# Weights decoded where they land, two blocks per pass, in a Nyström-attention and two-MoE-layer kernel

## The chip, the cores and the metric

One core of one Trainium2 chip. The metric is device time in microseconds (us) of one execution. Engines are named as the profile names them: PE (TensorE matmuls), PEld (its weight loads), DVE (VectorE), ACT (ScalarE), POOL (GpSimd), SP (SyncE, which here issues most DMAs). Each engine runs its instructions in the order of its own queue and waits there for the others.

## What is computed

Attention with 32 landmarks over 4 batches of 8 heads (576 positions, 64 wide), then two feed-forward layers over the 2304 tokens that come out of it. The weights of both layers arrive as 64-bit floats.

```python
A  = softmax(q @ k_lm.T);  Bm = softmax(q_lm @ k_lm.T);  C = softmax(q_lm @ k.T)
Z  = Bm.T / (norm1(Bm) * norminf(Bm))
for _ in range(6):
    Z = 2 * Z - Z @ Bm @ Z
x  = (A @ Z @ C @ v)                      # to 2304 x 512
h  = x @ moe_w_in                         # 512 x 2048
x  = (h * tanh(softplus(h))) @ moe_w_out  # 2048 x 512
h  = x @ moe2_w_in                        # 512 x 1024
solu = h * softmax(h)
out = (layernorm(solu) * g_ln) @ moe2_w_out
```

## The kernel before

**Stages.** The kernel first computes attention for batch 0 alone (the start-up), then walks 64 *pairs* of hidden blocks of the first layer, and last the second layer in 18 token tiles. A chunk is 288 tokens; a hidden block is 128 of the 2048 hidden columns; a pair is two blocks of one chunk. For each pair `gemm1` makes h from A transposed (AT) and u, `mish` applies the activation on ACT, `gsplit` splits the result in a high and a low part (gh on ACT, gl on DVE), and `gemm2` adds gh and gl times the rows of w_out into y, three pairs later (`LAG = 3`). h takes 12 matmuls a pair and y 24. The pairs go chunk 0 first half (pairs 1 to 4), chunk 1 (5 to 12), chunk 0 second half (13 to 16), then chunk after chunk; chunks 0 and 1 need batch 0 and chunk 2, from pair 17, needs batch 1.

**u.** `u_step(b, s)` multiplies W, the 64-wide end of batch b's attention, into a quarter s (512 hidden columns) of w_in: 8 matmuls into two PSUM tiles, a copy of each on ACT and a subtraction of each on DVE.

**Decoding.** [...] A block is 128 rows of 512 values: 32 blocks of the first layer, 16 of the second. A block is loaded into a staging tile, and goes through one pass on ACT (L145, the exponent) and three on DVE (L155, L158, L161, the shift, the sign and the low bits); w_out then takes a copy on ACT (L117) and a subtraction on POOL (L120). A staging tile is loaded again only after the block in it is decoded, eight blocks later for the first 20 blocks and three later after that. In this kernel the steps of the decoder are called from `w1_tick`: a few in the start-up, where `PSEQ` says `d`, and the rest spread over the first `DT = 8.5` pairs.

**Attention.** Batch 0 runs in the start-up in the order of the list `PSEQ` (q, k: transposes; e: the 32 by 32 softmax and the Newton steps for Z; c: the C part; a: the A part; w: W). Sums of q and k over 18 positions, the landmarks, are DVE reductions (L299), except in an `early` batch and group, where 18 matmuls with `fold` per operand do it (L323). The other groups run from `tasks`, one step at a time from `slot`, five slots a pair, from the slot and at the spacing that `PLAN` gives. In the kernel before, batch 1 group 0 begins in the start-up (x in `PSEQ`) and then waits for slot 39, and its later steps wait for the decoder.

**Second layer.** The decoder of its weights (`w2`) starts two chunks before the end of the pairs, with three staging tiles, and the steps come from `tick`. `split_y` splits the 18 input tiles, the low part on POOL.

## Time and profile before

| | us |
|---|---|
| median of 3 runs | 710.8 |
| lowest and highest run | 710.26, 710.86 |
| the profiled execution | 710.08 |
| span of the profiled execution | 708.2 |
| PE busy | 661.7 |
| DVE busy | 422.2 |
| ACT busy | 339.6 |
| POOL busy | 90.2 |

The span runs from the first to the last instruction; 1.9 us lie outside of it. All stages share one chain, so an engine that is busy 60% over the whole span may be the limit of one stage and idle in another: the profile is to be read by stage. The mean granted TensorE clock is 0.968 of full speed.

### The profile page before, as it was taken

What the parts mean: (1) busy time and instruction counts of PE and PEld (TensorE: products, weight loads), DVE (VectorE), ACT (ScalarE), POOL (GpSimd) and SP (SyncE); (2) the same over time, 40 slices, a digit from 0 to 9 for tenths busy, and PEclk for the clock granted to TensorE, in tenths of its full rate; (3) what the DMA queues carried; (4) which work ended last, traced back from release to release, by engine and by line L of the source; (5) the groups of instructions that cost most, each with busy time, mean ns of one, the idle gap of its engine ahead of it and who ended that gap; (6) DMA issues with size and microseconds to landing.
All of it is one profiled execution on the core that took longest, in us unless ns stands there. A gap on an engine that the chain in (4) does not pass through costs nothing.

```text
span 708.2 us, 12192 instructions
## 1 busy us (share of the span) xinstructions
PE 661.7 (93%) x4720; PEld 560.8 (79%) x4720; DVE 422.2 (60%) x1103; ACT 339.6 (48%) x658; POOL 90.2 (13%) x79
## 2 busy tenths in 40 slices
PE   4945999899999999999999989999999999999997
PEld 2634788788579989689989689998788888888885
DVE  6689799966365534364235784292876565656560
ACT  2435655765358474463264663461643434343331
POOL 0022232421000101000001151000210101010000
PEclk9867999989899999999999999999999999999999
DMA  9948636214210220030010453131211111111011
GB/s 245 227 123 273 125 89 179 95 51 118 68 52 17 69 68 1 34 103 1 1 34 2 164 192 110 34 109 34 75 45 44 46 46 44 45 46 30 16 31 44
DMA packets 43352, 55.44 MB, mean 78 GB/s; under 512 B 7712, under 2 KB 34848, under 8 KB 43296
## 3 DMA queue, kind: packets, MB, share of 16 engines
q1 hardware_dynamic: 38112, 49.37, 25.2%
q10 hardware_dynamic: 5184, 5.31, 2.2%
q8 instruction: 37, 0.61, 0.4%
q14 instruction: 19, 0.16, 0.1%
HBM read 44.63 MB, written 10.03 MB: 77 GB/s over the span
## 4 chain that ended last, share of the span: by engine, by line
PE 77%; DVE 12%; ACT 3%; DMA 3%; issue 2%; POOL 2%; SPq 0%; ACTq 0%; POOLq 0%
PE h L601 25%; PE y L653 23%; PE po L601 14%; PE pa L592 2%; PE pt L960 2%; PE pa L307 2%; PE pa L474 2%; DVE cw L161 1%; DVE gl L640 1%; DVE cw L158 1%; DMA sg<-in_moe_w_in_dram 1%; PE pa L425 1%; PE pa L336 1%; PE pa L323 1%; PE pa L413 1%
## 5 line engine op out<-in xcount | busy, mean ns | idle before, releaser
L601 PE MATMUL h<-AT,u 128*128 128x288 f32 x768 | 125.2, 307 | 6.9 <-ACT s L630 3.2
L601 PEld LDWEIGHTS h<-AT,u 128*128 128x128 f32 x768 | 109.0, 193 | 24.9 <-ACT u L595 7.4
L640 DVE TENSOR_TENSOR gl<-s,gh 128x288 fp32r<-128x288 f32 x128 | 57.7, 485 | 78.0 <-PE y L653 42.3
L601 PE MATMUL h<-vi_h,yb 128*128 128x512 f32 x288 | 93.7, 396 | 1.0 <-POOL yb L120 0.6
L653 PE MATMUL y<-gh,wo_h 128*128 128x288 f32 x512 | 89.0, 304 | 3.1 <-ACT ye L659 3.1
L653 PE MATMUL y<-gh,wo_l 128*128 128x288 f32 x512 | 83.7, 297 | 0.0
L653 PE MATMUL y<-gl,wo_h 128*128 128x288 f32 x512 | 81.9, 297 | 0.0
L653 PEld LDWEIGHTS y<-gh,wo_h 128*128 128x128 f32 x512 | 73.6, 189 | 9.7 <-ACT ye L659 5.3
L653 PEld LDWEIGHTS y<-gh,wo_l 128*128 128x128 f32 x512 | 72.6, 188 | 2.2 <-issue 2.1
L653 PEld LDWEIGHTS y<-gl,wo_h 128*128 128x128 f32 x512 | 71.9, 188 | 1.8 <-issue 1.8
L638 ACT ACTIVATE gh<-s 128x288 fp32r<-128x288 f32 x128 | 50.2, 436 | 38.8 <-PE y L653 38.5
L630 ACT ACTIVATE s<-h 128x576 f32<-128x576 f32 x64 | 41.6, 650 | 50.4 <-PE h L601 44.0
L601 PEld LDWEIGHTS h<-vi_h,yb 128*128 128x128 f32 x288 | 54.0, 188 | 12.8 <-POOL yb L120 1.1
L601 PE MATMUL po<-vo_h,lh 128*128 128x512 f32 x144 | 57.2, 397 | 0.0
L601 PE MATMUL po<-vo_l,lh 128*128 128x512 f32 x144 | 56.6, 393 | 0.0
L601 PE MATMUL h<-vi_l,yb 128*128 128x512 f32 x144 | 56.5, 392 | 0.0
L601 PE MATMUL po<-vo_h,ll 128*128 128x512 f32 x144 | 56.2, 391 | 0.0
L120 POOL TENSOR_TENSOR yb<-y,yb 128x512 fp32r<-128x512 f32 x18 | 23.4, 1304 | 208.5 <-ACT yb L117 208.5
L928 DVE TENSOR_REDUCE st<-h 128x1 f32<-128x1024 f32 x18 | 22.0, 1224 | 35.2 <-PE h L601 24.0
L117 ACT ACTIVATE yb<-y 128x512 fp32r<-128x512 f32 x18 | 11.3, 631 | 59.8 <-issue 54.6
L936 ACT ACTIVATE e<-s,st 128x1024 f32<-128x1024 f32 x18 | 20.7, 1152 | 30.6 <-DVE st L935 30.6
L596 DVE TENSOR_TENSOR u<-pa,u 128x512 fp32r<-128x512 f32 x32 | 21.0, 685 | 23.9 <-ACT u L595 23.7
(233 smaller groups left out, 1032.1 us busy)
## 6 DMA issues: line engine op xcount, KB each, us to landing
st_h<-in_moe_w_in_dram SPq DMA_DIRECT2D x18, 256.0 KB, 8.4
yd<-ye ACTq DMA_DIRECT2D x32, 144.0 KB, 1.9
y<-yd SPq DMA_DIRECT2D x18, 256.0 KB, 3.1
out_dram<-ob SPq DMA_DIRECT2D x72, 64.0 KB, 1.7
stage<-in_moe_w_out_dram SPq DMA_DIRECT2D x8, 512.0 KB, 3.4
sg<-in_moe_w_in_dram SPq DMA_DIRECT2D x8, 512.0 KB, 4.2
sg<-in_moe_w_out_dram SPq DMA_DIRECT2D x8, 512.0 KB, 3.7
q<-in_q_dram SPq DMA_DIRECT2D x6, 576.0 KB, 4.7
```

The source lines that it names most:

```text
L120: G.tensor_tensor(out=lo, in0=c, in1=f(hi), op=ALU.subtract)
L307: PE.transpose(pt[:, o], flat(src[:, 2 * i:2 * i + 2]), ident)
L474: PE.matmul(pz[:, c0:2 * L], lhsT=Z1, rhs=X1[:, c0:], start=True, stop=True)
L592: PE.matmul(po[g][h * L:(h + 1) * L], lhsT=wb[b][r, g, h * L:(h + 1) * L], rhs=wi_half(s // 2)[r, h, o], start=True, stop=True)
L596: V.tensor_tensor(out=u[:, 1, g, o], in0=po[g], in1=f(u[:, 0, g, o]), op=ALU.subtract)
L601: PE.matmul(o, lhsT=a, rhs=b_, start=i == 0, stop=i == n - 1)
L630: A.activation(out=s, in_=h, func=AF.Mish)
L638: A.activation(out=gh[:, e], in_=s[:, e], func=AF.Copy)
L640: V.tensor_tensor(out=gl[:, e], in0=s[:, e], in1=f(gh[:, e]), op=ALU.subtract)
L653: PE.matmul(yb[s_][d][:, 0:N], lhsT=w_out(s, i + e)[:, 0, d * P:(d + 1) * P], rhs=r[:, e], start=i == i0 and e == k == 0, stop=i + 2 == i1 ...
L928: V.tensor_reduce(out=st[:, 0:1], in_=h, op=ALU.max, axis=AX.X)
L936: A.activation(out=e, in_=s, func=AF.Square, bias=st[:, 4:5], accum_out=st[:, 5:6])
```

## The change

Every weight is now loaded into the tile in which its decoded parts will stand. A *unit* is two blocks, 128 by 1024 values: 16 units in the first layer (8 of w_in, 8 of w_out) and 8 in the second. There are no staging tiles; the first 12 units of the first layer are loaded at the start with nothing to wait for (w_out's all, w_in's first four), and w_in's last four follow when batch 0 has left the memory that it borrows. q, k and v of batch 0 lie in four tiles instead of two, so v comes in 24 loads instead of 12, half as large.

A unit takes two passes on ACT (L143, the exponent; L145, which takes the fourth byte of each low word and leaves its upper three bits) and two on DVE (L153 and L162), all 1024 wide. w_out then takes one copy on ACT (L213) and one subtraction on DVE (L222). The result buffer `dc` (`cc` in the second layer) has two tiles. POOL takes no part in decoding or in `split_y` any more: DVE makes the low parts.

Batch 0 group 1 and batch 1 group 1 join the `early` ones, whose landmark sums are matmuls. Batch 1 leaves the start-up: group 0 starts at slot 3, group 1 at slot 22, both 1.6 slots apart, and neither waits for the decoder. The decoder is spread over `DT = 10` pairs. The second layer's first four units are loaded once all u steps are done and decoded at 0.6 steps per block; two of the others are loaded in the last chunk and two after it.

```diff
-        if eng is None:
-            A.activation(out=hi, in_=c, func=AF.Copy)
-        else:
-            eng.tensor_copy(out=hi, in_=c)
-        G.tensor_tensor(out=lo, in0=c, in1=f(hi), op=ALU.subtract)
+    def split(hi, lo, c, eng=V):
+        A.activation(out=hi, in_=c, func=AF.Copy)
+        eng.tensor_tensor(out=lo, in0=c, in1=f(hi), op=ALU.subtract)
...
-            elif s == 1:
-                V.tensor_scalar(out=w, in0=w, scalar1=3, scalar2=0x7FFFFFF8,
-                                op0=ALU.logical_shift_left, op1=ALU.bitwise_and)
-            elif s == 2:
-                V.scalar_tensor_tensor(out=w, in0=t[:, :, :, 1], scalar=0x80000000, in1=w,
-                                       op0=ALU.bitwise_and, op1=ALU.bitwise_or)
-            else:
-                V.scalar_tensor_tensor(out=w, in0=t[:, :, :, 0], scalar=29, in1=w,
-                                       op0=ALU.logical_shift_right, op1=ALU.bitwise_or)
+                A.activation(out=cs[j], in_=t[:, :, 1].bitcast(F32), func=AF.Copy, scale=2.0 ** -112)
+                low = t.rearrange("p n w -> p (n w)").bitcast(U8).rearrange("p (n w) -> p n w", w=8)
+                A.activation(out=t[:, :, 0], in_=low[:, :, 3], func=AF.Copy, scale=2.0 ** -5, bias=-31.0 / 64)
...
+        for j in range(n + 1):
+            if j < n:
+                t, w = items[j][0], cs[j].bitcast(U32)
+                V.scalar_tensor_tensor(out=w, in0=w, scalar=3, in1=t[:, :, 0],
+                                       op0=ALU.logical_shift_left, op1=ALU.bitwise_or)
+                yield max(0, j - 1)
+            if j:
+                items[j - 1][3](cs.pop(j - 1))
+            start(j + 1)
+            yield j
+            if j < n:
+                o = items[j][1]
+                V.scalar_tensor_tensor(out=w if o is None else o.bitcast(U32), in0=t[:, :, 1], scalar=0x80000000,
+                                       in1=w, op0=ALU.bitwise_and, op1=ALU.bitwise_or)
+                items[j][2](cs[j])
+                yield j
...
+    def land(side, m):
...
+            for g in range(NG):
+                src = w1_in[g * HG * D:(g + 1) * HG * D, cs].rearrange("(h d) f -> d h f", d=D)
+                SP.dma_start(out=t[g * D:(g + 1) * D].rearrange("p (h n) w -> p h (n w)", h=2),
+                             in_=src[:, 2 * a:2 * a + 2].bitcast(U32))
...
-        early = (b, g) == (1, 0)
+        early = (b, g) in EARLY
...
-    DT = 8.5
+    EARLY = ((0, 1), (1, 0), (1, 1))
+    DT = 10
...
-    PLAN = {(b, g): ((39, 53, 97, 117, 169, 212)[2 * b + g - 2], (1.5, 1.5, 1, 2.5, 0.5, 1.5)[2 * b + g - 2]) for b in range(1, B) for g in range(NG)}
+    PLAN = {(b, g): ((3, 22, 97, 117, 169, 212)[2 * b + g - 2], (1.6, 1.6, 1, 2.5, 0.5, 1.5)[2 * b + g - 2]) for b in range(1, B) for g in range(NG)}
...
-        w1 = decode(w1_items(), stage1, cbuf1, lambda j: j - 8 if j < NW1 + NS else j - NS, VL, lambda j: (0, 0, 0, 0, 0, 0, 0, 0, 0, 0, 0, 1, 0, 0, 0, 0, 0, 0, 0, 0, 0, 1, 0, 0, 0, 0, 0, 1, 0, 0, 0, 0)[j])
+        w1 = decode(w1_items(), lambda: att.tile([P, R * D], F32, tag="dc", name="dc", bufs=2)[:, 0:2 * NQ])
...
-                while x[1] <= now and (x[0] > 1 or done >= (0 if x[2] < (1 if x[4] is soon else 9) else 29)):
+                while x[1] <= now:
```

PE ahead of the first h of the program, from batch 0's W (the product of zz, the last Newton matrix, and Cv or its place in scr) on. Before (L307 and L323 are the transposes and landmark sums of batch 1, L592 the u step, L601 the first h):

```order
L488 MATMUL pa<-zz,scr_h 128x128
L307 MATMUL pa<-ident,q 128x128 x9
L323 MATMUL pa<-Tq,fold 64x128 x18
L307 MATMUL pa<-ident,k 128x128 x9
L323 MATMUL pa<-Tk,fold 64x128 x18
L592 MATMUL pa<-wi_94,W 32x512 x8
L601 MATMUL h<-AT,u_602 128x288 x5
```

After (L452 is the C times v product, L528 W, L630 the u step, L639 h; the 23 are the rest of pair 1 and pair 2):

```order
L452 MATMUL pa<-scr_u_94 32x64 x2
L639 MATMUL h<-AT,u_598 128x288
L452 MATMUL pa<-scr_u_95,scr_u_94 32x64 x2
L528 MATMUL pa<-zz,scr_w_92 128x128
L630 MATMUL pa<-w_109,W 32x512 x4
L639 MATMUL h<-AT,u_598 128x288 x23
```

The four rows of batch 1 are gone from this place; the u step follows W with nothing between.

ACT among the first pairs. Before, between the gh of pair 4 and the mish of pair 5 (L145 and L117 are one block each; L630 is mish):

```order
L638 ACTIVATE gh<-s 128x288 x2
L145 ACTIVATE cw<-st_l 128x512
L117 ACTIVATE wo_h<-cw 128x512
L145 ACTIVATE cw<-st_l 128x512
L630 ACTIVATE s<-h 128x576
```

After, from the gh of pair 2 on (L143, L145 and L213 are one unit each, ro_ a unit of w_out, r_ and w_ one of w_in; L355 copies transposes of batch 1; the mish of pair 3 comes some ten rows later):

```order
L673 ACTIVATE gh<-s 128x288 x2
L143 ACTIVATE dc<-r_144 128x1024
L145 ACTIVATE r_144<-r_144 128x1024
L143 ACTIVATE dc<-ro_147 128x1024
L145 ACTIVATE ro_147<-ro_147 128x1024
L355 ACTIVATE Tq<-pa 128x512 x2
L213 ACTIVATE hl<-dc 128x2x512
L633 ACTIVATE u_692<-pa 128x512 x2
L143 ACTIVATE dc<-ro_153 128x1024
```

More and wider decoding passes now stand between the activations of neighbouring pairs, with batch 1's copies among them.

## Rows read from the trace of the kernel before

**Rows 1.** Windows by stage: stretch, then PE, PEld, DVE, ACT, POOL busy, PEclk, DMA, GB/s

```profile
48.70:66.70 18.00, 8.38 (x85) 6.94 (x83) 15.44 (x32) 9.17 (x19) 4.22 (x4) 0.62 0.63 205
...
77.40:111.50 34.10, 32.06 (x238) 29.66 (x238) 31.95 (x49) 21.86 (x45) 10.30 (x7) 1.00 0.34 88
111.50:209.20 97.70, 92.24 (x768) 75.06 (x767) 66.81 (x159) 56.24 (x110) 16.46 (x14) 0.93 0.30 89
...
500.00:708.20 208.20, 203.26 (x958) 167.16 (x956) 120.28 (x387) 77.56 (x138) 19.08 (x15) 1.00 0.16 41
```

**Rows 2.** Timeline of the start-up: start, length, engine, line, tiles, count [idle <-releaser]

```profile
47.62 0.28 ACT L491 ACTIVATE W<-pa 128x128 f32<-128x128 f32 x1 [0.32 <-PE pa L488]
...
48.26 0.46 DVE L454 TENSOR_TENSOR AT<-ATr,AT 128x288 fp32r<-128x288 f32 x1
...
52.91 0.68 DVE L161 SCALAR_TENSOR_TENSOR wi<-st_h,wi 128x512 uint32<-128x512 uint32 x1
...
58.98 3.90 PE L323 MATMUL pa<-Tq,fold 128*64 128x128 f32 x36
...
64.64 2.19 PE L323 MATMUL pa<-Tk,fold 128*64 128x128 f32 x36 [0.16 <-ACT Tk L317]
...
76.64 0.78 ACT L638 ACTIVATE gh<-s 128x288 fp32r<-128x288 f32 x2
```

**Rows 3.** Waits of SP's queue in 0 to 60 us: total, times, longest

```profile
SPq L135 <- DVE wi L161: 20.7, 3, 9.5
```

**Rows 4.** Groups by line and shape: operation, count | busy us, mean ns | idle before

```profile
L155 DVE TENSOR_SCALAR wi<-wi 128x512 uint32<-128x512 uint32 x16 | 7.4, 460 | 0.7 <-ACT wi L145 0.7
L161 DVE SCALAR_TENSOR_TENSOR wi<-stage,wi 128x512 uint32<-128x512 uint32 x4 | 2.8, 689 | 0.1
L145 ACT ACTIVATE wi<-st_h 128x512 f32<-128x512 f32 x9 | 6.0, 664 | 0.7 <-ACT ye L659 0.7
L117 ACT ACTIVATE wo_h<-cw 128x512 fp32r<-128x512 f32 x16 | 10.1, 629 | 13.1 <-DVE cw L161 13.1
L120 POOL TENSOR_TENSOR wo_l<-cw,wo_h 128x512 fp32r<-128x512 f32 x16 | 22.7, 1417 | 43.0 <-ACT wo_h L117 43.0
L299 DVE TENSOR_REDUCE scr_h<-scr_h 128x64 f32<-128x1152 f32 x1 | 2.1, 2139 | 0.0
```

**Rows 5.** The same view: operations 1024 wide, on DVE and on ACT

```profile
L933 DVE SCALAR_TENSOR_TENSOR s<-e,st,h 128x1024 f32<-128x1024 f32 x18 | 23.0, 1280 | 0.5
L936 ACT ACTIVATE e<-s,st 128x1024 f32<-128x1024 f32 x18 | 20.7, 1152 | 30.6 <-DVE st L935 30.6
```

**Rows 6.** The same view: what else ACT and DVE do for a pair

```profile
L630 ACT ACTIVATE s<-h 128x576 f32<-128x576 f32 x64 | 41.6, 650 | 50.4 <-PE h L601 44.0 <-DVE gl L640 5.9
L630 ACT ACT_TABLE_LOAD x14 | 18.0, 1283 | 2.5 <-DVE gl L640 1.8 <-ACT ye L659 0.6
L638 ACT ACTIVATE gh<-s 128x288 fp32r<-128x288 f32 x128 | 50.2, 436 | 38.8 <-PE y L653 38.5
L640 DVE TENSOR_TENSOR gl<-s,gh 128x288 fp32r<-128x288 f32 x128 | 57.7, 485 | 78.0 <-PE y L653 42.3 <-ACT gh L638 33.8 <-ACT s L630 1.3
L317 ACT ACTIVATE Tk<-pa 128x512 f32<-128x512 f32 x14 | 8.0, 597 | 13.5 <-PE pa L307 13.1
```

**Rows 7.** The chain that ended last: start, us, what; one of each kind

```profile
295.05 1.26 PE pa L592 x16
...
344.78 1.60 PE h L601 x12
346.38 3.19 PE y L653 x24
```

**Rows 8.** Timeline: the ends of h of pair 9 and of pair 21

```profile
110.39 1.20 PE L601 MATMUL h<-AT,u 128*128 128x288 f32 x7 [0.65 <-DVE u L596]
...
207.38 1.85 PE L601 MATMUL h<-AT,u 128*128 128x288 f32 x12
```

**Rows 9.** Timeline near the second layer's decoding: where PE waits

```profile
414.13 0.96 PE L653 MATMUL y<-gh,wo_h 128*128 128x288 f32 x4 [1.16 <-ACT ye L659]
...
417.82 0.84 PE L653 MATMUL y<-gh,wo_h 128*128 128x288 f32 x4 [1.53 <-ACT ye L659]
```

More of the change, by code (lines that the diff above doesn't have):

```diff
@@ L122, in decode @@
-    def decode(items, stage, cbuf, after, first=0, on_pool=lambda j: False):
-        n = len(items)
-        st, cs = {}, {}
-        def load(j):
-            if j < n:
-                t = stage(j, [P, *items[j][1], 2])
-                n_p = P // len(items[j][0])
-                for i, src in enumerate(items[j][0]):
-                    SP.dma_start(out=t[i * n_p:(i + 1) * n_p].rearrange("p a b w -> p a (b w)"), in_=src.bitcast(U32))
-                st[j] = t
+    NQ = 4 * P
+    NW = 2 * 2 * NQ
@@ new lines, in nystrom_moe_kernel, with words, w_in, w_raw @@
+    scr = {x: wip.tile([P, NW], F32, tag=x, name=f"scr_{x}") for x in ("w2", "w3", "u2", "u3")}
+    wi, wr, un, wo = {}, {}, {}, {}
+    def words(ap):
+        return ap.bitcast(U32).rearrange("p (n w) -> p n w", w=2)
+    def w_in(s):
+        if s not in wi:
+            wi[s] = wip.tile([P, NW], F32, tag=f"w{s}", name=f"w_{s}")
+        return wi[s]
+    def w_raw(s):
+        if s not in wr:
+            wr[s] = wip.tile([P, NW], F32, tag=f"u{s}", name=f"r_{s}")
+        return wr[s]
+    def u_q(s):
+        if s not in un:
+            un[s] = wip.tile([P, 2, NG, NQ], F32R, tag=f"u{s}", name=f"u_{s}")
+        return un[s]
@@ L170, in decode @@
         yield 0
         start(0)
-        for j in range(-1, n):
-            step(j, 2)
-            yield max(0, j)
-            start(j + 2)
-            step(j + 1, 0)
-            yield max(0, j)
-            step(j, 3)
-            while nl < n and after(nl) <= j:
-                load(nl)
-                nl += 1
-            yield max(0, j)
-            step(j + 1, 1)
-            if j >= 0:
-                items[j][2](cs.pop(j))
-                st.pop(j)
-            yield j + 1
-    O1, O2 = 1, 2
@@ L209, in nystrom_moe_kernel, with free_tag, drop @@
+    raw, tag_of, live = {}, {}, {"rv": 0, "dc": 0}
+    def free_tag():
+        return next((t for t in ("rv", "dc")[:1 + (done >= NU)] if live[t] < 2), None)
+    def drop(*key):
+        raw.pop(key)
+        if key in tag_of:
+            live[tag_of[key]] -= 1
     aw = {}
@@ L729, in nystrom_moe_kernel @@
         lim = 10 ** 6
+        for m in range(4, 8):
+            land("i", m)
         tasks = []
@@ L749, in slot @@
             now += 1
-            while ahead and len(raw) < RB - (done < 2 * NF):
+            while ahead and free_tag():
                 b, g, nm = ahead.pop(0)
@@ L822, in need @@
         def need(side, i):
-            while done <= pos[side, i] and done < 2 * NF:
+            while done <= pos[side, i] and done < NU:
                 w1_tick()
@@ L896, in nystrom_moe_kernel @@
                 if i == NH - 1:
[L897 to L899 removed]
+                    w2.append(decode2(vo_pairs((0, 1))))
                 if i == NF - 5:
@@ L971, in gemm4 @@
             for c in range(NF2):
-                pairs += [(lh[:, c], vo["h"][:, c]), (lh[:, c], vo["l"][c][:, 0]), (ll[:, c], vo["h"][:, c])]
+                vh, vl = (vo[c // 2][:, c % 2, x] for x in range(2))
+                pairs += [(lh[:, c], vh), (lh[:, c], vl), (ll[:, c], vh)]
             mm3(po, pairs)
@@ L1007, in nystrom_moe_kernel @@
                 split_y(t + 2)
-            spin(w2, 6 if t < L4 else 100)
+            for _ in range(3 if t < L4 else 100):
+                if w2 and next(w2[0], "end") == "end":
+                    w2.pop(0)
             if t >= L4:
```

283 lines of the change are left out of this document (135 added, 148 removed).

## The prediction

> **What bounds the kernel now.** I read the windows by stage first, then the groups by line, the chain of waits, and the timeline where a stage begins or ends. [rows 1] splits the program. From 48.7 to 66.7 us no engine is full: PE is busy 8.38 of 18.00 us, DVE 15.44, ACT 9.17, at a granted clock of 0.62. This is latency: W is there at 47.9 (47.62 + 0.28, [rows 2]), but SP waited 20.7 us for staging tiles [rows 3], so the fourth block of w_in is only decoded at 53.6, and batch 1's landmark matmuls (3.90 us at 58.98, 2.19 at 64.64, [rows 2]) stand on PE ahead of the u step. The first gh of a pair ends at 76.64 + 0.78 = 77.4. From there to 111.5 PE (32.06 of 34.10) and DVE (31.95) are both full, and ACT is at 21.86. From 111.5 to 209.2 PE is busy 92.24 of 97.70 at 0.93. From 500 on it is busy 203.26 of 208.20 at 1.00. So the start-up is order and latency, the first pairs are PE and DVE together, and the rest is PE. The change touches the first two and a little of the third.
>
> The profiled execution took 710.08 us; the sum is made against it. The median of the runs is 0.7 above, which I don't add.
>
> **Part 1: the start-up, gh of pair 1.** Four things leave PE's and DVE's way here: the wait for staging tiles, three of DVE's passes per block (0.46 + 0.69 + 0.69 us, [rows 4]), batch 1's transposes and sums, and landmark reductions of group 1 of batch 0 (two of 2.1 us on DVE [rows 4], which become matmuls on PE of 2.2 us, or 3.9 at the low clock, [rows 2]). I count the last as neutral. The first four w_in blocks are two units now, loaded before everything except q and k, and decoded long before W. After W at 47.9 and AT at 48.7 (48.26 + 0.46, [rows 2]) come eight u matmuls, two ACT copies of 0.60 [rows 6], h, a table load of 1.28, mish of 0.65 and two gh in 0.78 [rows 2, 6]; ACT also has two passes of a w_out unit ahead of mish, 2 x 1.15 [rows 5]. With 1.3 for u and 0.7 to 1 for h that is about 48 + 7.5 = 55.5. The low end is 52 (the w_out passes fall in a gap); the high end is 61 (a landmark matmul group at half clock, 3.9, and one more unit of decoding, 2.3, ahead of it). I take **55.5**, 22 us earlier than now. That is a head start and no gain yet: the decoding and batch 1 that stood in those 22 us are still to be done.
>
> **Part 2: what a unit costs.** Before, two blocks take 2 x (0.46 + 0.69 + 0.69) = 3.7 us of DVE and 2 x 0.66 of ACT; a unit of w_out 2 x 0.63 more of ACT and 2 x 1.42 of POOL [rows 4]. After, the two DVE passes are 1024 wide; the nearest row is L933 at 1.28, so 2.56, and for w_out a subtraction at about 1.3 more. ACT's passes go by L936, 1.15 each: 2.3, and 3.45 for w_out. L145 reads single bytes eight apart, which no row shows; between a plain 1.1 and twice the 512-wide pass, 1.33. Per unit DVE gains about 1.1 (w_out: 0.2 loses against it), ACT loses 1.0, POOL is empty. The relief goes to DVE and the load to **ACT**.
>
> **Part 3: gh of pair 1 to gh of pair 9.** I count what the order of the changed kernel puts between these two points. ACT: 34 wide passes x 1.15 = 39.1; 8 table loads x 1.28 = 10.3; 8 mish x 0.65 = 5.2; 16 gh x 0.39 = 6.3; 8 copies of u and of batch 1's transposes x 0.57 = 4.6 [rows 6]; some 24 small attention operations, by batch 0's own at about 0.45 each, 10.7. Sum **76**. DVE: 26 x 1.28 + 8 x 1.3 + 16 x 0.45 + 16 of small ones = 67. PE: 96 h matmuls (8 x 1.60), 5 pairs of y (16.0), 4 u steps (5.0), folds (3 x 2.2) and small transposes, 57 at full clock [rows 7]. So ACT becomes the bound of this stage, where it was at 64% [rows 1]. On top come stalls: `dc` is a ring of two, so ACT's first pass of a unit waits until DVE's second of the unit before the last (1.28 to 2.56 behind), and DVE's passes wait for ACT's byte pass. Queued behind ACT's wait are mish and gh of the pair, and PE's y waits for those. No row shows such a ring 1024 wide; the end below is 0 (it never closes), above 8 units in which one 1.28 pass and a bit is exposed, 13. I take 6, since DVE has 15 us to spare. Then gh of pair 9 is at 55.5 + 82 = **137.5**, and h of pair 9, 0.65 + 0.78 + about 0.55 earlier, at 135.5. Before, it ends at 110.39 + 1.20 = 111.6 [rows 8]. The change is 24 us late here, but batch 1 is then nearly done, and all of the decoding far ahead.
>
> **Part 4: pair 9 to pair 21.** Before: 111.6 to 207.38 + 1.85 = 209.2 [rows 8], 97.6 us for work of about 79: 12 x 1.60 of h, 11.5 x 3.19 of y, u steps, batch 1's matmuls. Its 18 us of loss are PE waiting for batch 1 before pair 17 and for the decoder. After, left in this stretch are 12 x 1.60 = 19.2 of h, 9 x 3.19 = 28.7 of y (y follows three pairs behind and less has been held back), 5 u steps x 1.26 = 6.3 [rows 7], the other batches' sums and transposes, some 2.7 + 10: **67**. Loss between 3 (all waits gone) and 14 (the u steps still wait for the last four w_in units); I take 6, a third of before, as one of its two waits is gone. So h of pair 21 ends at 135.5 + 73 = **208.5**, against 209.2: −0.7. Behind this point both kernels do the same work for the pairs.
>
> The last four w_in units are loaded behind 16.8 MB of q, k, v and weights; at the 205 GB/s of [rows 1] that has landed at about 84 us, and the first is decoded at some 97. Cover, with 13 us to spare; gone, it would cost the difference on the u step.
>
> **Part 5: the second layer.** Before, PE waits 1.16 and 1.53 us for ye near 414 [rows 9], where ACT stood behind a chain of copies and POOL's low parts. POOL is out, decoding is spread at 0.6 steps, so these waits go: −2.7, between 0 and −2.7. DVE takes the low parts: 120.28 of 208.20 busy [rows 1], so hidden; if they stand ahead of ye's subtraction the gain is lost. The token tiles from 500 on are PE-bound and keep their matmuls: 0.
>
> Sum: −0.7 − 2.7 = −3.4, **706.7 us**. Own range, from stalls, losses and the late term: 703 to 712.
>
> **Rivals.**
>
> *Slower: the starved PE runs at the low clock.* While PE waited in the start-up, its granted clock was 0.62 on average [rows 1], and the same 36 matmuls took 3.90 us there and 2.19 later [rows 2]. In pair 1 to 9 of the changed kernel, PE has 57 us of work in 82. If that is granted 0.62 too, it takes 92, ACT is no longer the bound, and the stage is 10 longer; some 3 to 4 more follow as pair 9 to 21 begins low. 706.7 + 13.5 = **720**. It decides below a mean clock of 57/82 = 0.70. Against it: PE is never idle for long there, and 111.5 to 209.2 held 0.93 with losses. The Trainium skill, "TensorE: Matmul & The Clock Gate", section "What's actually happening", says that "the default state is throttled, and activity releases the throttle", which agrees with 0.62 in the waiting start-up and 1.00 in [rows 1]'s full stretches. Chance 0.30.
>
> *Faster: no stall on ACT.* The ring never closes and DVE's spare time covers all: 76 instead of 82, and a loss of 3 instead of 6 from pair 9 to 21: −9, **698**. For it: DVE has 67 in 82. Chance 0.20.
>
> *Same: the late gain does not come.* DVE's low parts stand where POOL's stood, in front of ye, so −2.7 is lost and only −0.7 is left: **709.4**, up to 710. Chance 0.10.
>
> **How the numbers follow.** The forecast, 706.7, has 0.40; inside it, 0.75 is faster, 0.20 the same and 0.05 slower. A measurement of this kernel tells about 0.2% (1.4 us) from no change. Faster: 0.30 + 0.20 = 0.50; same: 0.08 + 0.09 = 0.17; slower: 0.02 + 0.30 + 0.01 = 0.33. The range goes from 697, just below the faster rival, to 721, just above the slower one.
>
> **What would show it.** First gh at 55.5 (52 to 61): part 1. ACT busy 90% or more and DVE about 80% between gh of pair 1 and of pair 9, which ends near 137.5: part 3; the wide ACT passes at 1.1 to 1.33 and DVE's at 1.28: part 2. A clock above 0.85 there speaks against the slower rival, one below 0.70 for it. h of pair 9 and 21 at 135.5 and 208.5: part 4. No PE wait for ye above 1 us near the second layer's decoding: part 5. From the last pairs on, the two traces should run in parallel, 208 us from token tile to end. I am wrong if the byte pass is far dearer than 1.33 (at 34 wide passes, a third of them, each 0.5 us more is 6 us on the bound engine), if w_in's last units come late, or if PE's losses from pair 9 on stay at 18, which gives 718.

## The result, and the profile after

The changed kernel takes 717.06 us (716.14 to 717.27), the kernel before 710.53 us beside it: 1.0089 times as long, with an interval of 1.0072 to 1.0107. It is 6.5 us slower where 3.4 us faster was forecast. The time lies inside the range, and the sign is wrong. The profiled execution took 716.14 us with a span of 714.4; before it was 708.2, so 6.2 us are to be found. Ratios leave out runs more than 1.5% above the fastest of their kernel; beside e5 to e8 these are 6 of the 17 runs of the kernel before, with clocks in the range of the others, so those four ratios stand some 0.3% too high (with all 17 runs e5 is 1.015, e6 1.019, e7 1.006 and e8 1.007).

The page of the changed kernel, busy time of the whole span, and PE's busy share and granted clock in 40 slices:

```profile
PE 669.7 (94%) x4848; PEld 572.4 (80%) x4848; DVE 391.0 (55%) x1033; ACT 364.9 (51%) x657; POOL 25.0 (3%) x34
...
PE   5885979699999999999999999999999999999997
...
PEclk9756889599999999999999999999999999999999
```

DVE is 31 us less busy than before, POOL 65 less, ACT 25 more. PE is 8 us *more* busy: it has 128 matmul records more, and its clock row is low in slices 2 to 6 and in slice 8, that is up to some 143 us; after that it stays full.

The places to compare are the beginnings of `mish` (ACT s of 576), one per pair. Timelines on ACT, the changed kernel first, then before: start, length, instruction. The rows are gh of pair 1, mish and gh of pair 9, mish of pair 21; then mish of 9 and of 21.

```profile
54.22 0.77 ACT L673 ACTIVATE gh<-s 128x288 fp32r<-128x288 f32 x2
...
146.39 0.65 ACT L665 ACTIVATE s<-h 128x576 f32<-128x576 f32 x1 [0.36 <-PE h L639]
...
147.42 0.78 ACT L673 ACTIVATE gh<-s 128x288 fp32r<-128x288 f32 x2
...
219.07 0.65 ACT L665 ACTIVATE s<-h 128x576 f32<-128x576 f32 x1 [1.40 <-PE h L639]
```

```profile
113.20 0.65 ACT L630 ACTIVATE s<-h 128x576 f32<-128x576 f32 x1 [2.80 <-DVE gl L640]
...
209.27 0.65 ACT L630 ACTIVATE s<-h 128x576 f32<-128x576 f32 x1 [1.39 <-PE h L601]
```

Pair 1 is 22 us early, pair 9 is 33 us late, pair 21 is 9.8 us late. Behind pair 21 the changed kernel gains: mish of pair 64 begins at 482.1 against 476.4, 5.7 us late, and the end is 6.2 late. So the whole loss is ahead of pair 21, and 3.6 us of it come back later.

Ahead of pair 21 both kernels do the same pairs: 252 matmuls of h, 408 of y and 128 of u in the records. (For a matmul of the landmark sums or of the bursts below the profile has two records: 36 for the 18 of a group, 16 for a burst of 8.) Windows by stage, the changed kernel up to its pair 21, then the kernel before up to its own (stretch; busy PE, PEld, DVE, ACT, POOL; granted clock; DMA):

```profile
0.00:30.00 30.00, 20.73 (x208) 15.00 (x208) 16.02 (x55) 13.09 (x26) 1.50 (x8) 0.97 0.74 192
30.00:53.30 23.30, 20.57 (x156) 12.43 (x156) 15.14 (x58) 9.99 (x22) 3.36 (x5) 0.50 1.02 300
53.30:81.00 27.70, 19.67 (x136) 16.95 (x137) 19.54 (x25) 21.57 (x32) 0.67 (x1) 0.71 1.04 293
81.00:115.00 34.00, 28.57 (x236) 25.92 (x235) 21.72 (x40) 32.61 (x50) 2.72 (x3) 0.90 0.21 55
115.00:146.40 31.40, 23.35 (x158) 19.05 (x157) 20.44 (x39) 14.78 (x22) 0.00 (x0) 0.73 0.28 79
146.40:219.10 72.70, 71.16 (x658) 59.28 (x657) 33.23 (x87) 37.44 (x80) 2.73 (x3) 1.00 0.16 47
```

```profile
0.00:48.00 48.00, 31.35 (x275) 20.57 (x276) 32.96 (x111) 15.78 (x39) 5.06 (x12) 0.87 0.90 219
48.00:75.60 27.60, 16.29 (x133) 10.46 (x131) 22.97 (x42) 13.87 (x27) 8.16 (x7) 0.69 0.77 213
75.60:113.20 37.60, 35.14 (x263) 32.32 (x256) 34.26 (x52) 23.65 (x49) 10.67 (x8) 0.99 0.40 103
113.20:209.30 96.10, 90.64 (x756) 73.58 (x756) 65.21 (x156) 56.28 (x111) 16.14 (x13) 0.93 0.29 87
```

Read PE's column. Up to pair 21 PE is busy 184.1 us after and 173.4 before, and it waits 35.0 after and 35.9 before. The waits are the same; the loss is busy time. Two things can make it, and each has an account.

The first is added work. Up to pair 21 PE has 1544 records after and 1416 before, since two more groups take their landmark sums from matmuls. Here are these sums (L323 before, L361 after) and the transposes that go with the sums on DVE (L310 before, L346 after) by themselves: stretch; busy PE, PEld; clock; DMA.

```profile
0.00:209.27 209.27, 6.08 (x72) 5.60 (x72) 0.89 0.51 137
0.00:219.07 219.07, 15.17 (x216) 13.81 (x216) 0.85 0.46 130
...
0.00:209.27 209.27, 4.54 (x32) 1.97 (x32) 0.89 0.51 137
0.00:219.07 219.07, 2.27 (x16) 0.99 (x16) 0.85 0.46 130
```

That is 17.4 us instead of 10.6, so 6.8 of the 10.7 us stand in these lines.

The second is the clock. Weigh each stretch's busy time by it: what the clock takes away (busy x (1 − clock), summed) is 25.8 us after and 15.8 before, 10.0 apart, and what is left, PE's work at full clock, is 158.3 and 157.6.

The two hardly fit together: 6.8 and 10.0 are more than 10.7, and the second leaves only 0.7 us for added work. The second takes a mean clock per stretch and lets a matmul's whole time go with it, but a group of 16 records takes 1.21 us at a clock of 0.50 and 0.71 at 1.00 (in e9 below), 1.7 times as long and not twice. So the accounts are good to some 6 us. They name two suspects, and the experiments had to show whether either is a cause.

Waits between pair 1 and pair 9 after the change (us in all, times, longest): PE waits for ACT, and DVE for PE.

```profile
DVE Z L299 <- PE pa L514: 6.6, 4, 4.2
...
PE h L639 <- ACT s L665: 6.3, 4, 4.1
...
PE pa L630 <- ACT Tq L355: 6.0, 2, 5.7
```

How such a wait looks, in timelines from the hole ahead of pair 9: first ACT, then PE.

```profile
125.73 1.15 ACT L143 ACTIVATE dc<-ro 128x1024 f32<-128x1024 f32 x1 [1.51 <-DVE hl L222]
126.78 0.58 ACT L355 ACTIVATE Tq<-pa 128x512 f32<-128x512 f32 x1
```

```profile
127.41 0.64 PE L433 MATMUL pa<-ident,Ce 128*32 128x128 f32 x4 [2.27 <-ACT Tq L355]
...
134.24 0.66 PE L514 MATMUL pa<-X,Z 128*128 128x64 f32 x2 [2.87 <-DVE Z L299]
...
135.47 2.06 PE L630 MATMUL pa<-w,W 64*32 64x512 f32 x16 [0.37 <-ACT Tq L355]
138.12 0.61 PE L639 MATMUL h<-AT,u 128*128 128x288 f32 x1 [0.59 <-ACT u L633]
138.85 4.11 PE L361 MATMUL pa<-Tq,fold 128*64 128x128 f32 x36
```

Decoding makes a 32-bit float of each 64-bit weight, and of w_out's a high and a low part. ACT waits for DVE with a pass of it in its hand, batch 1's copy Tq stands behind that pass, PE's next steps behind the copy, and the u step of pair 9 behind those. Then the 36 records of a landmark group take 4.11 us where such a group took 2.19 in [rows 2], and the u step 2.06 where it took 1.26 in [rows 7].

### The profile page after: what moved, and what is told of

Read it like the earlier page. It is cut to its first block, busy times and chain, and to the rows that moved or that the text cites. A ratio compares the mean times of both kernels' runs of the same rounds, so it can differ in the third digit from the quotient of the medians.

```text
span 714.4 us, 12232 instructions
## 1 busy us (share of the span) xinstructions
PE 669.7 (94%) x4848; PEld 572.4 (80%) x4848; DVE 391.0 (55%) x1033; ACT 364.9 (51%) x657; POOL 25.0 (3%) x34
## 4 chain that ended last, share of the span: by engine, by line
PE 80%; ACT 8%; DVE 6%; DMA 3%; issue 2%; SPq 0%; POOL 0%; ACTq 0%; POOLq 0%; DVEq 0%
PE h L639 26%; PE y L688 24%; PE po L639 14%; PE pa L630 3%; PE pt L979 2%; PE pa L343 2%; PE pa L514 2%; PE pa L361 2%; DVE dc L153 1%; DMA r<-in_moe_w_in_dram 1%; PE pa L452 1%; DMA scr_u<-in_k_dram 1%; ACT dc L143 1%; ACT L665 1%; PE pa L465 1%
## 5 line engine op out<-in xcount | busy, mean ns | idle before, releaser
L688 PE MATMUL y<-gh,hl 128*128 128x288 f32 x1024 | 162.1, 303 | 0.6 <-ACT ye L694 0.4
L688 PEld LDWEIGHTS y<-gh,hl 128*128 128x128 f32 x1024 | 143.8, 191 | 10.6 <-issue 7.2
L639 PE MATMUL h<-AT,u 128*128 128x288 f32 x768 | 127.4, 311 | 9.9 <-ACT s L665 6.3
L639 PEld LDWEIGHTS h<-AT,u 128*128 128x128 f32 x768 | 111.1, 197 | 26.1 <-ACT u L633 11.5
L639 PE MATMUL h<-hl,yb 128*128 128x512 f32 x432 | 103.5, 394 | 1.2 <-DVE st L948 0.9
L639 PEld LDWEIGHTS h<-hl,yb 128*128 128x128 f32 x432 | 79.7, 188 | 17.9 <-DVE yb L126 1.3
L639 PE MATMUL po<-hl,lh 128*128 128x512 f32 x288 | 88.9, 390 | 0.0
L688 PE MATMUL y<-gl,hl 128*128 128x288 f32 x512 | 80.9, 296 | 1.3 <-DVE gl L675 1.3
L688 PEld LDWEIGHTS y<-gl,hl 128*128 128x128 f32 x512 | 71.8, 188 | 3.2 <-issue 1.7
L639 PEld LDWEIGHTS po<-hl,lh 128*128 128x128 f32 x288 | 53.9, 188 | 11.1
L639 PE MATMUL po<-hl,ll 128*128 128x512 f32 x144 | 56.1, 390 | 0.0
L630 PE MATMUL pa<-w,W 64*32 64x512 f32 x256 | 30.4, 686 | 8.2 <-ACT Tq L355 6.0
L955 ACT ACTIVATE e<-s,st 128x1024 f32<-128x1024 f32 x18 | 20.7, 1151 | 29.9 <-DVE st L954 29.8
L639 PEld LDWEIGHTS po<-hl,ll 128*128 128x128 f32 x144 | 27.0, 188 | 5.6
```

The source lines that it names most:

```text
L630: PE.matmul(po[g][h * L:(h + 1) * L], lhsT=wb[b][r, g, h * L:(h + 1) * L], rhs=w[r, h], start=True, stop=True)
L639: PE.matmul(o, lhsT=a, rhs=b_, start=i == 0, stop=i == n - 1)
L688: PE.matmul(yb[s_][d][:, 0:N], lhsT=w_out(s, i + e)[:, d * P:(d + 1) * P], rhs=r[:, e], start=i == i0 and e == k == 0, stop=i + 2 == i1 an ...
L955: A.activation(out=e, in_=s, func=AF.Square, bias=st[:, 4:5], accum_out=st[:, 5:6])
```

## The experiments

Each ratio is to the kernel before, run beside it on the same chip, with its 95% interval. "Pair n" is the begin of mish of pair n in the profiled execution, "PE waits" and "PE busy" go up to mish of pair 21, and "bursts" is what added matmuls take of the busy time. Single executions spread by some us here, so marks are read only where they differ by more. The changed kernel itself has four runs, within 1.1 us; beside the experiments the kernel before alone spread over 8 to 15 us, and they ran on three chips. A difference to the changed kernel is therefore read only from some 3 us on.

| run | ratio | pair 1 | pair 9 | pair 21 | PE waits | PE busy | bursts |
|---|---|---|---|---|---|---|---|
| before | 1 | 75.6 | 113.2 | 209.3 | 35.9 | 173.4 | |
| after | 1.0089 [1.0072, 1.0107] | 53.3 | 146.4 | 219.1 | 35.0 | 184.1 | |
| e1 batch 1 late | 1.0062 [1.0036, 1.0088] | 54.3 | 114.2 | 218.5 | 29.1 | 189.4 | |
| e2 no byte pass | 1.0004 [0.9979, 1.0028] | 55.2 | 141.3 | 214.1 | 32.8 | 181.3 | |
| e3 five units first | 1.0181 [1.0140, 1.0221] | 57.2 | 125.6 | 227.8 | 35.3 | 192.5 | |
| e4 DT = 16 | 1.0171 [1.0104, 1.0239] | 54.6 | 162.7 | 225.2 | 41.0 | 184.2 | |
| e5 one early group | 1.0180 [1.0127, 1.0232] | 64.1 | 157.8 | 227.3 | 42.0 | 185.3 | |
| e6 low part on POOL | 1.0219 [1.0169, 1.0269] | 57.0 | 152.9 | 225.7 | 38.9 | 186.8 | |
| e7 batch 1 middle | 1.0093 [1.0061, 1.0124] | 53.6 | 119.8 | 214.1 | 30.7 | 183.4 | |
| e8 DT = 8.5 | 1.0101 [1.0058, 1.0143] | 53.8 | 129.0 | 217.6 | 31.4 | 186.2 | |
| e9 bursts of 8 | 1.0078 [1.0039, 1.0116] | 81.5 | 143.6 | 220.1 | 19.7 | 200.4 | 39.0 |
| e10 third DVE pass | 1.0081 [1.0046, 1.0116] | 54.9 | 148.7 | 221.2 | 37.5 | 183.7 | |
| e11 byte pass on POOL | 1.0152 [1.0112, 1.0193] | 55.3 | 150.4 | 223.1 | 38.9 | 184.2 | |
| e12 before, early groups | 1.0038 [1.0007, 1.0070] | 79.8 | 117.3 | 213.9 | 34.5 | 179.4 | |
| e13 bursts of 2 | 1.0077 [1.0035, 1.0119] | 60.5 | 144.3 | 217.2 | 30.3 | 186.9 | 13.4 |
| e14 bursts of 4 | 1.0041 [1.0006, 1.0076] | 60.5 | 141.4 | 214.0 | 26.9 | 187.1 | 20.7 |
| e15 bursts of 2, middle | 0.9977 [0.9945, 1.0009] | 59.9 | 117.7 | 212.2 | 27.9 | 184.3 | 11.7 |
| e16 before, bursts of 2 | 1.0012 [0.9979, 1.0044] | 75.1 | 114.1 | 207.9 | 30.9 | 177.0 | 12.0 |
| e17 bursts of 4, middle | 1.0014 [0.9981, 1.0047] | 61.5 | 115.9 | 210.6 | 23.8 | 186.8 | 20.7 |
| e18 as e17, no byte pass | 1.0026 [0.9995, 1.0056] | 65.0 | 118.7 | 214.2 | 23.3 | 190.9 | 20.9 |

**Where batch 1 stands (e1, e7).**

```diff
-    PLAN = (3, 22, 97, 117, 169, 212), (1.6, 1.6, 1, 2.5, 0.5, 1.5)
+    PLAN = (55, 68, 97, 117, 169, 212), (1.0, 1.0, 1, 2.5, 0.5, 1.5)    e1
+    PLAN = (22, 40, 97, 117, 169, 212), (1.6, 1.6, 1, 2.5, 0.5, 1.5)    e7
```

> Batch 1's attention starts at slots 55 and 68 (pairs 12 and 14, spacing 1.0) instead of 3 and 22; nothing else changes. Theory (queues): the changed kernel loses its time where batch 1's small steps and the decoding passes share PE's, ACT's and DVE's queues, from mish of pair 2 to 3 (25 us) and of 8 to 9 (32 us), and no engine is full there. Then mish of pair 9 comes at about 120 instead of 146.4, and what is lost later at pair 17 is less than that: mish of pair 21 at 209 to 214, total 707 to 712. Rival (load): the work only moves, PE and ACT are as busy in pairs 11 to 17 as before: pair 9 at 125 but pair 21 at 219 again, total 716 to 717. Rival (clock): the low clock in pairs 2 to 9 stays, since the start-up is no fuller: pair 9 no earlier than 138.

> Batch 1 starts at slots 22 and 40 instead of 3 and 22, same spacing. Theory (PE's own work and its clock): PE's work up to pair 21 is the same, and the waits only change places: pair 21 within 3 us of 219, total 714 to 718. Rival (queues): without batch 1 in pairs 1 to 4 the first hole (25 us from mish of pair 2 to 3) becomes 18, and group 1's chain, after the decoding, meets no passes: total 708 to 713.

In e1 pair 9 comes at 114.2, 32 us earlier, as the theory of the queues had it. But a new hole opens ahead of pair 17 (mish of pair 16 at 163.4, of 17 at 200.8), pair 21 is where it was, and the gain in the total is not clear of nothing. e7 gains nothing that is clear of the noise either (its profiled execution is the fastest of its runs, 4 us below their median). So the holes are made by batch 1's chain, and they move with it. The first form of my theory, that batch 1 stands in the wrong place, falls. In e1 PE also waits 6 us less and is busy 5 us longer with as many records (1544).

**How the decoder is spread (e3, e4, e8).**

```diff
-        lim = 3
+        lim = 5      (and six more d in PSEQ)     e3
-    DT = 10
+    DT = 16                                       e4
+    DT = 8.5                                      e8
```

> The start-up decodes five units instead of three, so w_in's units 2 and 3 are ready before pair 1 and the u step of pair 3 need not wait for a burst of decoding. 4 ACT passes (4.5 us) and 4 of DVE (4.9 us) move ahead of W, where ACT was busy 18.7 of 48 us and DVE 27.8. Theory (queues): the first hole, mish of pair 2 to 3, shrinks from 25 to 12 to 17 us, pair 9 comes 5 to 10 earlier, total 708 to 713; W comes 0 to 3 later. Rival (load): 4.5 us of ACT less, total 712 to 713. Rival (second hole alone decides): pair 3 earlier, pair 9 at 146 as before, total 716 to 717.

> DT = 16 instead of 10: the decoder is spread over 16 pairs, as far as needs do not force it. About 4 of the units 3 to 15 move from before pair 9 to after it: 4 x 3.45 = 14 us of ACT and 4 x 3.7 = 15 of DVE. Theory (queues): the second hole, mish of pair 8 to 9 (32 us), loses the passes that batch 1's chain waits behind, pair 9 at 128 to 138, pair 21 at 210 to 216, total 707 to 714. Rival (load): as much as is taken away comes back after pair 9, total 716 to 717. Rival (batch 1's chain of hand-overs alone is long enough): pair 9 at 143 to 146, total 715 to 717.

> DT = 8.5, as in the kernel before, instead of 10. With 16 it became 5 us slower. Theory (batch 1's k of group 1 can only be loaded into the decoder's second buffer once decoding is over: SP waits 16.5 us for L222, and the load is issued at 132.2): the load is issued 5 to 10 earlier, and pair 9 or 11 follows, total 712 to 715. Rival (the load on ACT): ACT's passes are denser, pairs 3 to 8 later, total 717 to 720.

e3 and e4 are both some 6 us slower than the changed kernel, against what I expected of them; e8 cannot be told from it. In e3 the hole ahead of pair 9 shrinks from 32 to 12 us, and one of 44 us stands between mish of pair 10 and 11 (128.2 and 172.4). In e4 the hole ahead of pair 9 grows from 32 to 53 us (109.5 to 162.7), where 12 wide passes of ACT stand in it and 9 did before. So spreading the decoding further does not help; that batch 1's chain meets the passes there all the same is my reading of it.

**The byte pass (e2, e10, e11).** e2 replaces what it gives by a constant zero.

```diff
-                A.activation(out=t[:, :, 0], in_=low[:, :, 3], func=AF.Copy, scale=2.0 ** -5, bias=-31.0 / 64)
+                (left out; L153's in1 is zero)                                               e2
+                (left out; L153 shifts and masks, a third STT takes t[:, :, 0] >> 29)        e10
+                G.tensor_scalar(out=t[:, :, 0], in0=low[:, :, 3], scalar1=2.0 ** -5, ...)    e11
```

> The byte pass L145 on ACT is left out, and DVE's L153 takes a constant zero in its place, so the low three bits of each weight are missing. 16 passes of 1.12 us leave ACT, 13 of them between gh of pair 1 and of pair 9 (14.5 us). Theory (queues): ACT has 24 us idle there, so at most a third of that comes back: pair 9 at 140 to 146, total 713 to 717. Rival (load on ACT, the bound my sum took): pair 9 comes 12 to 15 earlier, at 132, total 704 to 707. Rival (clock): PE waits less, the clock rises a little, pair 9 at 138.

> The byte pass L145 leaves ACT, and DVE takes the low three bits itself: three passes 1024 wide (shift and mask, low bits, sign) where there are two, so nothing is left out. ACT loses 16 passes of 1.13 us in the first layer, DVE gains 16 of 0.9 to 1.25. Theory (ACT's load, by the run without the byte pass, which came 6 us earlier): DVE was idle 30 of 93 us from pair 1 to pair 9, so most of the 6 us comes: total 711 to 714. Rival (hand-overs): DVE's longer queue makes ACT wait for dc as often, total 715 to 718. Rival (DVE becomes the bound): pair 9 at 150 or later, total 719 to 722.

> The byte pass is on POOL, which is idle, instead of ACT: 16 passes leave ACT, POOL takes them at 2.4 to 3 us each. Theory (ACT's load): total 711 to 714, if DVE isn't slowed. Rival (POOL beside DVE slows both, as L162 took 1.99 us instead of 1.22 beside POOL's low parts): DVE's passes reach 1.6 to 2 us, and DVE waits for POOL's 2.4 us instead of ACT's 1.13: total 718 to 724.

Without the pass 5 to 6 us come back (1.0089 to 1.0004; medians 717.1 and 712.2), a third of the 18 us that its 16 passes in the first layer take on ACT, and 5.0 us of it ahead of pair 21. Moved to DVE it gains nothing, and on POOL it loses. The pass is one link of the hand-overs. Where another engine has it, ACT waits for that: ahead of the exponent pass and of w_out's copy it stands idle 6.4 us up to 230 us in the changed kernel, 17.4 in e10 and 17.0 in e11. In e11 the shift pass L153 on DVE is slower too, 1.34 to 1.67 us on the mean of a group instead of 1.22.

**The other parts (e5, e6, e12).**

```diff
-    EARLY = ((0, 1), (1, 0), (1, 1))
+    EARLY = ((1, 0),)                                                          e5
-                V.tensor_tensor(out=x[:, :, 1], in0=c, in1=f(x[:, :, 0]), op=ALU.subtract)
+                G.tensor_tensor(out=x[:, :, 1], in0=c, in1=f(x[:, :, 0]), op=ALU.subtract)    e6
-        early = (b, g) == (1, 0)                                               (kernel before)
+        early = (b, g) in ((0, 1), (1, 0), (1, 1))     (and another PSEQ)      e12
```

> Only batch 1 group 0 stays early, as in the kernel before: the landmark sums of batch 0 group 1 and of batch 1 group 1 are DVE reductions again. PE loses 144 fold matmuls (8.8 us at full clock, 72 of them in batch 0's start-up) and gets 16 matmuls of L346 back (about 5); DVE gets four reductions of 2.1 us. Theory (PE's own work: up to pair 21 PE is idle as long in both kernels, 35 us, and busy 10.6 us longer): pair 21 comes 3 to 6 us earlier, total 711 to 714. Rival (hand-overs through DVE): DVE's reductions stand between decoding passes, the holes grow, total 718 to 722. Rival (neutral, as the sum counted it): 716 to 718.

> The low part of w_out (L222) is on POOL again, for all units that go unscaled: DVE loses 8 passes of 1.22 us in the first layer, POOL gets 8 of about 2.4 to 2.8. Theory (in-order hand-overs on DVE): ACT and PE wait for DVE where L222 stands in front (1.51 us at 125.7, 2.9 for Z at 134): pair 9 comes 2 to 5 earlier, total 713 to 716. Rival (PE's own work): no change, 716 to 718. Rival (DVE and POOL slow each other): DVE's passes beside POOL's longer than 1.28 us, total 718 to 721.

> The kernel before with one part of the change alone: batch 0 group 1 and batch 1 group 1 take their landmark sums from matmuls too (group 1's four steps of q and k stand where its three stood). In the changed kernel taking this part away cost 6 us of the total and 10.8 at pair 1. Theory (it is a gain of its own, through DVE's reductions and the matmuls that raise the clock): pair 1 comes 4 to 8 earlier, pair 21 2 to 6, total 705 to 709. Rival (the start-up before waits for staging and the decoder anyway): pair 1 within 2 us, total 709.5 to 712. Rival (PE's own work): total 712 to 715.

Two parts of the change are gains where they stand: undoing the early groups makes it 4 to 6 us slower, undoing the low part on DVE 7 to 9. In the kernel before, the early groups lose 0.4%, PE is busy 6.0 us longer and pair 21 comes 4.6 us later, as the rival by PE's own work had it (712 to 715 expected, 714.1 measured). But e12 is not the early groups alone: its `PSEQ` also takes all of group 1's steps of q and k to the front, as in the changed kernel, where three of each stood spread out. In e5 pair 1 comes 10.8 us later, with 64 records of matmuls fewer up to there, so the number of PE's matmuls is not what sets the start-up; and up to pair 21 PE has the 128 records fewer, is no less busy (185.3 us) and waits 7 us more. The added landmark matmuls cost PE time, but taking them out of the changed kernel does not bring the loss back.

**The clock (e9, e13 to e18).** Bursts of matmuls that nothing reads stand between the steps of batch 0's start-up (n = 8 in e9, 2 in e13 and e15, 4 in e14, e17 and e18; e15, e17 and e18 have e7's `PLAN`, e18 also e2's edit; e16 is the kernel before with n = 2). There are 20 of them, 19 in e16, not the 30 and 17 of the expectations.

```diff
+            if nm == "f":
+                bank_n[0] += 1
+                pf = ps_y.tile([P, 512], F32, tag=f"y{bank_n[0] % 4}", name="pf")
+                for i in range(n):
+                    PE.matmul(pf[0:D, 0:P], lhsT=fold, rhs=ident, start=i == 0, stop=i == n - 1)
```

> About 30 bursts of 8 matmuls that nothing reads (fold by ident, 64x128) stand between the steps of batch 0's start-up, from the Newton steps to W: some 14.6 us of PE work at full clock (2.19 us for 36). Theory (the low clock is a cause): in the changed kernel the granted clock is 0.50 from 30 to 50 us, and a group of 16 takes 1.21 us there and 0.71 at 22 us; with the bursts the clock stays near 1.00 up to pair 1, the matmuls on the chain take 10 us less, most of the bursts lie in PE's waits for DVE, and mish of pair 1 comes at 49 to 54 although work was added; total 709 to 716. Rival (the low clock is only a sign of waiting): the added work stands on the chain, pair 1 at 60 to 66, total 724 to 730.

In e9 the clock stands at 1.00 through the start-up. One group of the chain, L465 of group 1 of batch 0, in the timeline of the changed kernel and then of e9, and what the bursts cost there (group by line, up to pair 21):

```profile
34.60 1.21 PE L465 MATMUL pa<-scr_w,scr_w 64*32 64x288 f32 x16
```

```profile
51.78 1.96 PE L740 MATMUL pf<-ident,fold 128*64 128x128 f32 x16
53.67 0.71 PE L465 MATMUL pa<-scr_w,scr_w 64*32 64x288 f32 x16
...
L740 PE MATMUL pf<-ident,fold 128*64 128x128 f32 x320 | 39.0, 276 | 0.0
```

The same 16 matmuls take 0.71 us instead of 1.21. My price for the bursts was far too low (14.6 us expected for 30 of them, 39.0 measured for 20, since one of 8, 16 records, takes 1.96), so pair 1 comes 28 us later. Yet pair 21 is only 1 us later, and the total is the same. PE's busy time without the bursts is 161.4 us up to pair 21, 23 less than in the changed kernel, near the 25.8 of the account by the clock; and PE waits 15 us less. 39 us of useless work were paid for by the clock and by waits.

> As the run with bursts of 8 matmuls in the start-up, but bursts of 2 (0.49 us by that run's 1.96 for 8): some 10 us of PE work instead of 39. There the clock stood at 1.00 to the end, PE's useful work up to pair 21 took 161 us instead of the changed kernel's 184, and the end was the same because the bursts and PE's remaining waits cost as much as that gave. Theory (time up to pair 21 is PE's work at its clock plus its waits): if 2 are enough to hold the clock, pair 1 comes at 50 to 60, pair 21 at 200 to 212, total 696 to 708; if the clock falls all the same, pair 1 at 58 to 62 and total 716 to 722. Rival (another chain, ACT's and DVE's decoding or batch 1's loads, sets pair 21 whatever PE does): 715 to 718 with either clock.

> Bursts of 4 (0.98 us, some 20 us in all). Theory (PE's work, clock and waits): if the clock holds, half of the bursts' cost of the run with 8 is gone, pair 21 at 204 to 216, total 700 to 712. Rival (another chain sets pair 21): 715 to 718.

> Bursts of 2 in the start-up, and batch 1 at slots 22 and 40. Theory (PE's work, clock and waits): the hole from pair 2 to 3 had its low clock with batch 1's matmuls in it; without them pairs 1 to 8 run densely. Pair 9 at 110 to 120, pair 21 at 204 to 212, total 700 to 708. Rival (another chain, batch 1's, sets pair 21): 711 to 716 as with batch 1 in the middle alone.

> The kernel before with the same bursts of 2 in its start-up (17 places). Its granted clock was 0.62 from 48 to 67 us and it lost some 15 us up to pair 21 by the clock. Theory (PE's work, clock and waits): if the clock holds, pair 1 comes at 70 to 75 instead of 75.6 in spite of 8 us more work, total 702 to 709. Rival (its start-up waits for staging and the decoder): pair 1 at 76 to 82, total 711 to 716.

> Bursts of 4 in the start-up, and batch 1 at slots 22 and 40. Bursts of 2 with the middle place gave 0.9977 of before, bursts of 4 alone 1.0041. Theory (PE's work, clock and waits): the clock is near 1.00 at pair 1 with 2 already, so 4 only add work: pair 1 at 60 to 62, pair 21 at 210 to 214, total 706 to 710, 0.995 to 1.000 of before. Rival (the dose still matters, since with 2 the clock dipped at 52 and again after pair 9): pair 21 at 206 to 209, total 702 to 705.

> The same, with the byte pass L145 left out (a constant zero instead, so the low three bits of each weight are missing). Left out of the changed kernel it gave 6 us. Theory (ACT's passes cost by making PE wait, which lowers its clock): with the clock up and batch 1 out of the first pairs PE waits only 4 us from pair 1 to 9, so 0 to 3 us come. Rival (ACT's load has a price of its own): 5 to 7 us again, total 700 to 704.

e13 is the miss: with bursts of 2 the clock falls again behind the start-up (0.82 from pair 1 to 9), and nothing is gained. e14 gains some 3 us over the changed kernel, less than expected, and the two intervals just meet. The clear pair is e7 against e15: the same order of batch 1, and with 11.7 us of useless matmuls *added* the kernel is 0.8 to 1.2% faster, 0.9977 against 1.006 to 1.0093, with intervals apart. (In the two profiled executions pair 21 differs by 1.9 us only, e7's being its fastest.) More work on PE, less time: up to pair 21 PE's busy time without the bursts is 172.6 us in e15 and 183.4 in e7. In that arrangement the low clock is a cause and not a sign. Windows show the stage from pair 1 to pair 9, first in e7 and then in e17 (second of its three rows). With bursts its clock is 1.00 instead of 0.90, nearly the same matmuls keep PE busy 51.73 us instead of 57.31, and it takes 54.40 us instead of 66.20. The changed kernel's 93 us hold a good part of batch 1 besides (525 records for 423).

```profile
53.60:119.80 66.20, 57.31 (x423) 47.99 (x424) 40.90 (x53) 50.58 (x75) 0.68 (x1) 0.90 0.57 157
```

```profile
0.00:61.50 61.50, 49.97 (x526) 38.85 (x528) 37.45 (x118) 26.64 (x53) 4.85 (x13) 1.00 0.89 260
61.50:115.90 54.40, 51.73 (x430) 45.28 (x434) 35.32 (x48) 43.60 (x68) 0.67 (x1) 1.00 0.54 137
115.90:210.60 94.70, 85.07 (x763) 68.72 (x762) 53.35 (x135) 53.04 (x104) 5.55 (x6) 0.93 0.19 54
```

Behind pair 9 it falls to 0.93, where batch 1's chain now stands, and the larger dose bought nothing over e15. e18 answers the byte pass: with the clock up and batch 1 out of the first pairs, leaving it out gains nothing (1.0026 against 1.0014), where it gained 5 to 6 us in e2. So its price depends on what stands around it and is not its own length; that it is a price of PE's waits fits, but whether the bursts or the place of batch 1 took it away was not run. e16 gains nothing in the kernel before. No run is clearly faster than the kernel before; e15 (0.9977, up to 1.0009) comes nearest.

Two things stay open. The bursts also move PE's steps against each other (in e15 pair 1 comes 6 us later than in e7, and the u copies of the second quarter at the same time, 69.0 and 69.1 us), and I have no run that raises the clock without adding work. So how the 6.5 us divide between lower clock, longer hand-overs and the added landmark matmuls is not shown: only the two accounts say it, and they do not agree. And which single wait lowers the clock was not tried.

## Why the prediction was wrong

**Part 1 held.** gh of pair 1 ends at 54.22 + 0.77 = 55.0; 55.5 was forecast. Some of that is luck: at a clock of 0.50 the u step took 1.93 us for 1.3 and h 3.01 for at most 1, but W came 0.6 us early and ACT's two w_out passes and table load hid the rest. That this is a head start and no gain was right: pair 9 comes 33 us late. e9 gives 28 us of it away and ends the same, though there the clock pays for it.

**Part 2 held.** The passes of a unit, changed kernel, by line and shape (count; busy, mean ns; idle before and its releasers):

```profile
L153 DVE SCALAR_TENSOR_TENSOR dc<-dc,ro 128x1024 uint32<-128x1024 uint32 x8 | 9.8, 1221 | 3.9 <-ACT ro L145 3.8
L222 DVE TENSOR_TENSOR hl<-dc,hl 128x1024 fp32r<-128x1024 f32 x8 | 9.8, 1220 | 1.7 <-ACT hl L213 1.7
L162 DVE SCALAR_TENSOR_TENSOR dc<-ro,dc 128x1024 uint32<-128x1024 uint32 x8 | 9.7, 1215 | 0.1
L145 ACT ACTIVATE ro<-ro 128x1024 uint32<-128x1024 uint8 x8 | 9.3, 1163 | 0.0
L143 ACT ACTIVATE dc<-ro 128x1024 f32<-128x1024 f32 x8 | 9.3, 1159 | 3.7 <-DVE w L162 2.2 <-DVE hl L222 1.5
L213 ACT ACTIVATE hl<-dc 128x1024 fp32r<-128x1024 f32 x8 | 8.5, 1059 | 2.7 <-DVE dc L162 2.6
```

1.22 us on DVE (1.28 taken), 1.16 and 1.06 on ACT (1.15 taken); reading bytes eight apart costs nothing extra, the low end of what was allowed.

**Part 3 is the step that failed.** From gh of pair 1 to gh of pair 9 it gave 82 us, ACT's 76 plus 6 of stalls, as if one engine were the bound. The stage took 148.2 − 55.0 = 93.2. From mish to mish ACT is busy 69.0 of 93.1, DVE 61.7 and PE 71.6: no engine is the bound. ACT's work was over-counted by some 7 us, and its stalls are 24 us, four times the 6 taken and beyond the bound of 13. That bound counted the ring of `dc` alone, and the ring costs little. ACT's waits between pair 1 and pair 9 (us in all, times, longest), the costliest and then the two for `dc`:

```profile
ACT Tq L362 <- PE pa L361: 6.7, 2, 4.4
...
ACT dc L143 <- DVE w L162: 2.2, 1, 2.2
...
ACT dc L143 <- DVE hl L222: 1.5, 1, 1.5
```

In all ACT stands 16.1 us for PE and 6.5 for DVE, 3.7 of them for `dc`. The sum left out that ACT also waits for PE, that batch 1's chain goes through PE, ACT and DVE in turn, and that its hand-overs stand behind passes of 1.1 to 1.2 us on two of them. ACT above 90% was the sign I named for being right; it is 74%.

**The slower rival had the mechanism, not the form.** It took PE's 57 us at a clock of 0.62 and asked whether they exceed 82, which they would below 0.70. The clock is 0.79 there, above that point, and PE's busy time 71.6 is near 57/0.79 = 72. That agreement is luck in part: the 57 had y of 5 pairs and 4 u steps, but 8 pairs of y (192 records, 24 a pair) and 2 u steps (32 records, 16 each) stand in the stretch, 9.6 us more and 2.5 less by [rows 7]. Parts 3 and 4 together had y of 14 pairs, and 17 were done by pair 21. And the slow work and the waits are not parallel, of which the longer counts: PE waits 21.5 us beside it, and both together are the 93. Its 720 is 3 us above the result. What I held against it, that PE is never idle for long, is not so: it waits 5.7, 4.1 and 2.9 us at a time.

**Part 4 held, its split did not.** From pair 9 to pair 21 73 us were forecast, and 72.7 measured, with PE busy 71.16 and hardly any waits (67 and 6 forecast). The 6 came from a misreading: the kernel before does not wait 18 us there, as [rows 1] has PE busy 92.24 of 97.70 us, 5.5 us idle, and the rest of the 18 was slower or uncounted work. So pair 21 comes late by what part 3 was off.

**Part 5 held.** From mish of pair 49 to that of pair 63 the lag shrinks from 10.6 to 7.6 us, by 2.9; 2.7 were forecast, from the two waits for ye in [rows 9]. What is left of them in the changed kernel (PE's waits from 380 to 480 us):

```profile
PE y L688 <- ACT ye L694: 0.2, 1, 0.2
```

The stretch from pair 64 to the end is 0.5 us longer, where 0 was forecast. Not forecast were 0.8 us more lag from pair 21 to 49 and 2.0 less from 63 to 64. The sum closes: +9.8 − 4.1 from pair 21 to pair 64 + 0.5 = +6.2.

**The early groups** were counted as neutral, and they are not: PE's lines for them are 6.8 us longer, e5 says 4 to 6 us of gain in the changed kernel, and e12 nearly 3 of loss in the kernel before, with the other order. By e5 that term is not the one that turned the sign.
